# Output sums copied by ScalarE, one transposed load in place of two, and word conversions in another order, in a fused mLSTM and feed-forward kernel

## Chip, cores and metric

The kernel runs on one core of one Trainium2 chip. Its time is in device microseconds. Three runs of the kernel before gave 425.68, 427.31 and 429.06 us; the median is 427.31 us.

## What is computed

An mLSTM cell (4 batches, 8 heads, 768 positions, head size 40), followed by a feed-forward block on its output, laid out as 3072 tokens by 320.

```python
for t in range(S):                       # mLSTM, S = 768, state C (40x40) and n (40) per head
    m_new = np.maximum(f_gate[:, :, t] + m, i_gate[:, :, t])
    f_stab = np.exp(f_gate[:, :, t] + m - m_new)
    i_stab = np.exp(i_gate[:, :, t] - m_new)
    C = f_stab * C + i_stab * outer(vt, kt)
    n = f_stab * n + i_stab * kt
    h_tilde, nq = C @ qt, n @ qt
    y[:, :, t] = sigmoid(o_gate[:, :, t]) * h_tilde / np.maximum(np.abs(nq), 1.0)

h = ((x @ w1) * (x @ w2)) @ w3           # x: y as (3072, 320); w1, w2: 320 x 1024; w3: 1024 x 1024
out = h @ w_out                          # w_out: 1024 x 320
```

The four weights arrive as 64-bit floats, the other inputs as 32-bit floats.

## The kernel before

**Units and steps.** The sequence is cut into units of 128 positions of one batch: 24 units, numbered `n`, four batches to a chunk of positions. One step `s` of the loop at L820 does the scores and the state of unit `s` and the outputs of unit `s - 1`; besides, it does part of the feed-forward block. There are 32 steps; from step 25 on only feed-forward work is left. TensorE's instructions stay in the order of the program (`in_order`, L84), and so do those of the other engines (`keep_order`, L549): an instruction that waits holds up all that stand behind it on its engine.

**The cell.** `quarter_work` (L338) issues the products of a step in quarters of 64 positions: `ph` (weights times values, of unit s - 1), `pi` (queries times the state before), `ss` (scores of unit s) and `pc` (the state's update). They live in two pairs of PSUM banks, `cell`. `outputs` (L419) scales `pi` by a gate into `h` (L423), adds the four quarters of `ph` to it on VectorE (L430), takes max(|nq|, 1) and its reciprocal (L438 to L441), and makes y with the tanh of the output gate (L443, L445); its small operations are spread over the step by `den()`. L397 multiplies scores by the weights `pw`; L404 and L414 update the state, with POOL's `decayed` (L333) between them.

**Weights of the cell.** `pw` starts as a row of U, spread over partitions: by `rows_of_u` (L293, a VectorE transpose) for units below 10, by DMA (`load_u`, L155) after. `weights` (L298) takes eight exponentials on ScalarE, `masks` (L305) masks on POOL, `out_gate` (L269) takes the tanh.

**Keys and queries.** `turn` (L311) turns them: on TensorE with copies by ScalarE (L325) for units below 10, by VectorE's 32x32 transposes (L317) from 10 on. For these, `load_turned` (L141) loads each of the keys' and queries' halves twice, the second time shifted by 32 columns, so that the dimensions 32 to 39 lie where the transposes read: eight DMAs a step, on SP's queue.

**64-bit words.** `fetch` (L211) brings a piece of weights as words; `scale` (L187) scales its two halves on ScalarE (L191, L195), and `to_f32` (L197) joins them on VectorE (L199, L200). `scale_next` and `convert` (L233, L237) take the pieces in the order in which they were fetched. w1 and w2 are cut in two parts of 512 columns, each with their last 64 rows in `wr`. The first part is wanted by step 2, the second (`wr` last) by step 4. In step 3, `rest` (L883) issues two `scale_next`, and `convert` is called twice inside `quarter_work` (`late`, L376 and L409).

**Feed-forward.** `x_trans` (L478) turns y on TensorE for units below 15, after `twice` (L475) has doubled its last 64 columns on POOL. For later units y goes to DRAM and back (`send` L451, `get_back` L462) and is turned by VectorE (`x_turn` L468). `up` (L618) makes pa = x w1 and pb = x w2 for two slices of 128 columns, `up_rest` (L631) adds the last 64 rows and multiplies; its first block is issued in step 2, one in each of the steps 2 to 5, then two. The last three groups of tokens go by seven products instead of eight (`up_by_seven`, L668), whose banks in steps 19 to 24 are those of the cell. w3 and w_out are folded into one matrix in steps 9 to 16 (`w3_mm`, L259), which `ffn_out` and `out_by_seven` apply.

**Step 2.** The part `between` (L892) turns y of the units 0 and 1 and starts `up`. Between the two, `warm(1, small=38)` (L97) issues products of the identity, nobody reads them: one of 128x512 and 38 of 64x64.

PSUM tiles other than `cell` go round four banks (`mps`, L77): the fifth tile asked for waits until the first has been read.

## Time and profile before

| what | value |
|---|---|
| median of three runs | 427.31 us |
| runs | 425.68, 427.31, 429.06 us |
| the profiled execution's span | 425.8 us |
| TensorE's granted clock, mean | 0.996 |
| TensorE idle, 0 to 23 us | 4.5 us |
| TensorE idle, 23 to 60 us | 2.0 us |
| TensorE idle, 60 to 360 us | 2.1 us |
| TensorE idle, 360 us to the end | 3.4 us |
| VectorE's adds of ph (L430), 88 | 28.6 us, 326 ns each |
| ScalarE busy | 150.1 us |
| POOL busy | 154.3 us |
| DMA packets under 512 B | 109360 of 135211 |

The idle times are the lengths of the stages less TensorE's busy time in them. The profiled execution's span is close to the lowest of the three runs, 1.5 us under their median. Busy time of TensorE is modelled from starts of pipelined products, so a busy TensorE needn't be at its peak; where it waits, the line in the order of time names what it waited for in brackets.

### The profile page before, as it was taken

How to read it: one execution, taken by the hardware profiler on the slowest of the kernel's cores; microseconds unless marked ns; L12 is line 12 of the kernel's file. 1: busy time of each engine (PE TensorE's matmuls, PEld its weight loads, DVE VectorE, ACT ScalarE, POOL GpSimd, SP SyncE). 2: the span in 40 equal slices, each digit the busy share in tenths (PEclk: the TensorE clock that was granted, in tenths of full speed). 3: DMA queues.
4: the chain of work that ended last, by engine and by line, in shares of the span. 5: the costliest groups of instructions: out<-in, count | busy, mean ns of one | idle time of the engine just before them, and what ended most of it. 6: DMA issues, size and time to landing. Idle time of an engine off the chain costs nothing.

```text
span 425.8 us, 13079 instructions
## 1 busy us (share of the span) xinstructions
PE 414.1 (97%) x5353; PEld 335.3 (79%) x5353; DVE 313.5 (74%) x635; ACT 150.1 (35%) x404; POOL 154.3 (36%) x211
## 2 busy tenths in 40 slices
PE   7989989999999999999999999999999999999996
PEld 4768878888688788787777778788778879888896
DVE  6676986888949779778736966596868699575971
ACT  4766865567723623630433313032311110210000
POOL 4421342233303303303307751546453587542100
PEclk9989999999999999999999999999999999999999
DMA  8999998598977776985425675756421120000001
GB/s 186 204 173 245 214 144 140 134 193 180 215 183 154 166 182 135 181 164 105 89 80 130 153 141 121 142 133 117 87 44 36 35 39 2 31 2 31 2 32 62
DMA packets 135211, 51.15 MB, mean 120 GB/s; under 512 B 109360, under 2 KB 126960, under 8 KB 135152
## 3 DMA queue, kind: packets, MB, share of 16 engines
q1 hardware_dynamic: 131552, 46.29, 53.9%
q10 hardware_dynamic: 3600, 4.03, 2.7%
q8 instruction: 42, 0.69, 0.7%
q14 instruction: 17, 0.14, 0.1%
HBM read 44.50 MB, written 5.80 MB: 118 GB/s over the span
## 4 chain that ended last, share of the span: by engine, by line
PE 53%; issue 20%; DVE 7%; POOL 7%; SPq 7%; DMA 5%; ACT 1%; POOLq 0%; DVEq 0%
PE cell L92 17%; PE pa L92 12%; PE o L92 8%; PE pb L92 8%; PE p L92 3%; POOL pw L308 3%; SPq L184 3%; DVE w3T L666 2%; PE pt L95 1%; POOL vw L330 1%; SPq L148 1%; DMA raw<-in_moe_w_dram 1%; PE fill L92 1%; POOL raw L659 1%; POOL state L335 1%
## 5 line engine op out<-in xcount | busy, mean ns | idle before, releaser
L335 POOL TENSOR_TENSOR state<-state,decay 128x164 f32<-128x164 f32 x40 | 20.0, 500 | 154.8 <-DVE state L404 129.0
L92 PE MATMUL pa<-xT,w 128*128 128x256 f32 x240 | 60.4, 382 | 0.0
L92 PEld LDWEIGHTS pa<-xT,w 128*128 128x128 f32 x240 | 44.4, 190 | 6.8 <-DVE h L430 0.4
L303 ACT ACTIVATE pw<-pw,aT 128x64 f32<-128x64 f32 x184 | 46.4, 339 | 3.2 <-ACT o_sb L741 1.9
L92 PE MATMUL pb<-xT,w 128*128 128x256 f32 x192 | 45.4, 379 | 0.0
L729 POOL TENSOR_TENSOR ab<-ab,a_sb 128x512 f32<-128x512 f32 x22 | 29.4, 1356 | 32.2 <-DVE ab L684 32.2
L92 PEld LDWEIGHTS pb<-xT,w 128*128 128x128 f32 x192 | 36.4, 190 | 5.0
L711 POOL TENSOR_TENSOR wo<-wo 128x512 f32<-128x512 f32 x22 | 27.4, 1268 | 29.8 <-DVE wo L686 29.8
L92 PE MATMUL pa<-xT,wr 64*64 64x256 f32 x384 | 37.0, 386 | 0.5 <-DVE wr L200 0.5
L92 PE MATMUL wp<-wo,w3T 128*128 128x320 f32 x128 | 35.9, 433 | 1.1 <-DVE ab L639 0.6
L308 POOL TENSOR_SCALAR_AFFINE_SELECT pw<-pw 64x512 f32<-64x512 f32 x48 | 35.8, 746 | 3.0 <-ACT pw L303 1.2
L92 PE MATMUL pb<-xT,wr 64*64 64x256 f32 x384 | 36.4, 380 | 0.0
L92 PE MATMUL cell<-w3o,ab 128*128 128x320 f32 x128 | 35.4, 432 | 0.0
L638 ACT ACTIVATE a_sb<-pa 128x512 f32<-128x512 f32 x24 | 14.3, 598 | 59.0 <-PE pb L92 59.0
L639 DVE TENSOR_TENSOR ab<-pb,a_sb 128x512 f32<-128x512 f32 x24 | 16.4, 688 | 23.2 <-ACT a_sb L638 22.8
L92 PEld LDWEIGHTS wp<-wo,w3T 128*128 128x128 f32 x128 | 23.8, 190 | 10.5 <-DVE ab L639 0.8
L92 PEld LDWEIGHTS cell<-w3o,ab 128*128 128x128 f32 x128 | 24.3, 190 | 9.5
L92 PEld LDWEIGHTS pa<-xT,wr 64*64 64x64 f32 x384 | 18.9, 132 | 15.4 <-issue 8.8
L686 DVE SCALAR_TENSOR_TENSOR a_sb<-pa,wo 128x512 f32<-128x512 f32 x12 | 8.3, 689 | 29.8 <-PE pa L92 29.8
L430 DVE TENSOR_TENSOR h<-cell,h 64x164 f32<-64x164 f32 x88 | 28.6, 326 | 1.6
L92 PE MATMUL po<-w3o,ab 128*128 128x320 f32 x96 | 26.4, 433 | 0.0
L92 PEld LDWEIGHTS po<-w3o,ab 128*128 128x128 f32 x96 | 18.1, 190 | 7.3
(180 smaller groups left out, 846.4 us busy)
## 6 DMA issues: line engine op xcount, KB each, us to landing
raw<-in_moe_w_dram SPq DMA_DIRECT2D x64, 128.0 KB, 3.4
kbuf<-in_k_dram SPq DMA_DIRECT2D x24, 160.0 KB, 4.5
v_all<-in_v_dram SPq DMA_DIRECT2D x24, 160.0 KB, 4.9
o_in<-in_o_gate_dram SPq DMA_DIRECT2D x24, 160.0 KB, 4.8
pw<-U_d SPq DMA_DIRECT2D x28, 128.0 KB, 3.5
raw<-in_moe_w_dram SPq DMA_DIRECT2D x5, 512.0 KB, 6.7
raw<-in_moe_w_out_dram SPq DMA_DIRECT2D x8, 320.0 KB, 4.1
gates<-in_k_dram SPq DMA_DIRECT2D x28, 80.0 KB, 2.5
```

The source lines that it names most:

```text
L92: in_order(nc.tensor.matmul(out, lhsT=lhsT, rhs=rhs, start=start, stop=stop))
L184: nc.sync.dma_start(out=dst, in_=src)
L303: nc.scalar.activation(out=pw[:, h, :], in_=src[:, h, :], func=AF.Exp, bias=aT[:, c, b * H + h:b * H + h + 1])
L308: nc.gpsimd.affine_select(out=pw[r], in_=pw[r], compare_op=OP.is_ge, fill=0.0, base=0, pattern=[[0, H], [1, L]], channel_multiplier=-1)
L335: nc.gpsimd.tensor_tensor(out=new, in0=old, op=OP.mult, in1=decay[:, b * NP:(b + 1) * NP, 2 * c + x:2 * c + x + 1] .to_broadcast([P, NP, D1]))
L430: nc.vector.tensor_tensor(out=part, in0=ph[x][halves[e]], in1=part, op=OP.add)
L638: nc.scalar.mul(out=a_sb, in_=pa, mul=UP ** -2)
L639: nc.vector.tensor_tensor(out=ab_t[gr][j][:, fs[0]:fs[-1] + 1, t0:t0 + a_sb.shape[-1]], in0=pb, in1=a_sb, op=OP.mult)
L666: nc.vector.tensor_tensor(out=dst, in0=p, in1=q, op=OP.subtract)
L686: nc.vector.scalar_tensor_tensor(out=out, in0=p, scalar=UP ** -2, in1=q, op0=OP.mult, op1=OP.add)
L711: aside_by.tensor_tensor(out=kept[j][:, 1:4:2], in0=kept[j][:, 1:3], in1=kept[j][:, 3:4].to_broadcast([128, 2, TH]), op=OP.add)
L729: aside_by.tensor_tensor(out=t[:, f:FO:FH, :], in0=t[:, f:FO:FH, :], in1=a, op=OP.mult)
```

## The change

1. The filler in step 2 is two products of 128x512, and the 38 small ones are gone. `rows_of_u(3)` goes from ahead of the scalings to behind the three conversions there.
2. In step 3 the two scalings and two conversions go from inside the step's work to behind the next unit's turn, exponentials, masks and the gate.
3. For units from 10 on, ScalarE copies the four quarters of `ph` to `h`, VectorE scales `pi` into memory of `y` and adds both once. The ones beside the values are twos; the denominator is max(-r, r) of r = 1/(2 nq), cut at 0.5, in all units.
4. `load_turned` loads once (four DMAs); `shift` copies the eight last dimensions on ScalarE. The memory of those columns is cleared on POOL at step 4.
5. y is stored to DRAM in rows as it stands, by two DMAs in place of four, and read back in pieces of 32 floats in place of 96; the turn writes in another order.
6. w_out's words are joined by POOL, not by VectorE.
7. `x_trans` comes at the end of a step in all steps, ahead of the exponentials; before, from unit 7 on, it came at the start of the next step. In steps 16 to 23 the next unit's exponentials and the gate are issued ahead of the step's quarter work.

```diff
-    def warm(n, m=4, small=0):
+    def warm(n, m=4):
...
-        for i in range(small):
-            r = halves[i % 2]
-            mm(bank[r, 0, 0:L], ident[r, 0:L], ident[r, 0:L])
...
-    N_DIAG = 2
+    N_DIAG, N_OWN = 2, 10
...
-                for j in range(2):
-                    p0, c0 = hip * DP + j * 32, (1 - j) * 32
-                    nc.sync.dma_start(out=dst[p0:p0 + 32, c0:c0 + NP * RAW].rearrange("r (p e) -> r p e", p=NP),
-                                      in_=of.rearrange("p (r f) d -> r p (f d)", f=4))
+                nc.sync.dma_start(out=dst[hip * DP:hip * DP + 32, 32:TB].rearrange("r (p e) -> r p e", p=NP),
+                                  in_=of.rearrange("p (r f) d -> r p (f d)", f=4))
+
+    def shift(n):
+
+        for mem in turned_in[n % 2]:
+            e = mem[:, 32:TB].rearrange("r (g d) -> r g d", d=D)
+            for p0 in (0, DP):
+                nc.scalar.copy(out=e[p0 + 32:p0 + 64, :, 0:D - 32], in_=e[p0:p0 + 32, :, 32:D])
...
-            to_f32(dst, raw)
+            to_f32(dst, raw, nc.gpsimd if dst.shape[-1] == DM else nc.vector)
...
+        before = y[:, 0:H * D1].rearrange("p (h d) -> p h d", d=D1) if n >= N_OWN else h
...
-        for x, e in quarters if n >= N_DIAG else ():
+        if n >= N_OWN:
+            for x, e in quarters:
+                nc.scalar.copy(out=h[halves[x], 0:H // 2] if x == e else h[halves[x], H // 2:H], in_=ph[x][halves[e]])
+        for x, e in quarters if N_DIAG <= n < N_OWN else ():
...
+            if n >= N_OWN:
+                yield
+                V.tensor_tensor(out=h, in0=before, in1=h, op=OP.add)
+                V.reciprocal(out=den, in_=h[:, :, D:D1])
+            else:
+                yield V.reciprocal(out=den, in_=h[:, :, D:D1])
+            yield V.scalar_tensor_tensor(out=den, in0=den, scalar=-1.0, in1=den, op0=OP.mult, op1=OP.max)
+            v = h[:, :, 0:D]
+            yield V.scalar_tensor_tensor(out=v, in0=den.to_broadcast([P, H, D]), scalar=0.5, in1=v, op0=OP.min, op1=OP.mult)
+            yield V.scalar_tensor_tensor(out=y[:, 0:DM].rearrange("p (h d) -> p h d", d=D), in0=o_t.pop(n), scalar=1.0,
+                                         in1=v, op0=OP.add, op1=OP.mult)
...
+        nc.sync.dma_start(out=y_d[n][:, 0:DM], in_=y[:, 0:DM])
+        nc.sync.dma_start(out=y_d[n][:, DM:DM + REM], in_=y[:, KF * P:DM])
...
-        while s >= N_DVE and turned < min(s - 2, NY):
-            x_trans(turned)
-            turned += 1
...
-            if s == 3:
-                scale_next()
-                scale_next()
...
-            rows_of_u(3)
             for _ in range(3):
                 scale_next()
             for n in range(2):
                 x_trans(n)
                 if n == 0:
-                    warm(1, small=38)
+                    warm(2)
             for _ in range(3):
                 convert()
+            rows_of_u(3)
...
+        if NY < s < NU:
+            if s < NU - 1:
+                weights(s + 1)
+            out_gate(s)
         gated = None
         if s <= NU:
-            gated = quarter_work(s, rest, between if s == 2 else None, convert if s == 3 else None)
+            gated = quarter_work(s, rest, between if s == 2 else None, None)
...
+                shift(s + 1)
                 gated = turn(s + 1)
...
+        if s == 3:
+            scale_next()
+            scale_next()
+            convert()
+            convert()
...
+            nc.gpsimd.memset(gates[RG:P, 0:5 * TC], 0.0)
```

More of the change, by code (lines that the diff above doesn't have):

```diff
@@ L127 @@
     KC = KF + 1
-    y_d = [dram.tile([P, 4, KC, 32], FP, name=f"y_d{n}") if n >= NY else None for n in range(NU)]
+    y_d = [dram.tile([P, KC * P], FP, name=f"y_d{n}") if n >= NY else None for n in range(NU)]
     o_t, u_t = {}, {}
@@ L195, in scale, with to_f32 @@
             nc.scalar.activation(out=lo, in_=lo, func=AF.Copy, scale=2.0 ** -29, bias=2.0 ** 23)
-    def to_f32(dst, raw):
-        bits, V = dst.bitcast(U32), nc.vector
-        V.tensor_scalar(out=bits, in0=raw[:, :, 1], scalar1=3, scalar2=None, op0=OP.logical_shift_left)
-        V.tensor_tensor(out=bits, in0=bits, in1=raw[:, :, 0], op=OP.add)
+    def to_f32(dst, raw, adder):
+        bits = dst.bitcast(U32)
+        nc.vector.tensor_scalar(out=bits, in0=raw[:, :, 1], scalar1=3, scalar2=None, op0=OP.logical_shift_left)
+        adder.tensor_tensor(out=bits, in0=bits, in1=raw[:, :, 0], op=OP.add)
     def cols(c0, n):
@@ L241, in convert @@
         if dst is not None:
-            to_f32(dst, raw)
+            to_f32(dst, raw, nc.gpsimd if dst.shape[-1] == DM else nc.vector)
             return
         w3 = wst.tile([128, CW], FP, name="w3", tag="w3")
-        to_f32(w3, raw)
+        to_f32(w3, raw, nc.vector)
         if half == 0:
@@ L422, in outputs @@
         h = sb.tile([P, H, D1], FP, name="h", tag="h")
-        nc.vector.tensor_tensor(out=h.rearrange("p (n two) d -> p two n d", two=2), in0=pi,
+        y = y_t[n] = sb.tile([P, DM + REM], FP, name="y", tag="y")
+        before = y[:, 0:H * D1].rearrange("p (h d) -> p h d", d=D1) if n >= N_OWN else h
+        nc.vector.tensor_tensor(out=before.rearrange("p (n two) d -> p two n d", two=2), in0=pi,
                                 in1=gT[:, c, hs].rearrange("p (n two) -> p two n", two=2).unsqueeze(3)
@@ L437, in steps @@
             V = nc.vector
-            yield V.tensor_scalar(out=den.bitcast(U32), in0=h[:, :, D:D1].bitcast(U32), scalar1=0x7FFFFFFF, scalar2=None,
-                            op0=OP.bitwise_and)
-            yield V.tensor_scalar(out=den, in0=den, scalar1=1.0, scalar2=2.0, op0=OP.max, op1=OP.mult)
-            yield V.reciprocal(out=den, in_=den)
-            e = o_t.pop(n)
-            nc.vector.scalar_tensor_tensor(out=e, in0=e, scalar=1.0, in1=den.to_broadcast([P, H, D]), op0=OP.add, op1=OP.mult)
-            y_t[n] = sb.tile([P, DM + REM], FP, name="y", tag="y")
-            yield nc.vector.tensor_tensor(out=y_t[n][:, 0:DM].rearrange("p (h d) -> p h d", d=D), in0=h[:, :, 0:D],
-                                           in1=e, op=OP.mult)
+            if n >= N_OWN:
[9 more added lines that the diff above has]
+                                         in1=v, op0=OP.add, op1=OP.mult)
         done = steps()
@@ L454, in send @@
         y = y_t.pop(n)
-        for cc in range(KF):
-            nc.sync.dma_start(out=y_d[n][:, :, cc, :], in_=y[:, cc * P:(cc + 1) * P].rearrange("t (i c) -> t i c", c=32))
-        for i in range(0, 4, 2):
-            nc.sync.dma_start(out=y_d[n][:, i:i + 2, KF, :], in_=y[:, KF * P:DM].rearrange("t (i c) -> t i c", c=32))
+        nc.sync.dma_start(out=y_d[n][:, 0:DM], in_=y[:, 0:DM])
+        nc.sync.dma_start(out=y_d[n][:, DM:DM + REM], in_=y[:, KF * P:DM])
     back_t = {}
@@ L464, in get_back @@
         for i in range(4):
-            nc.sync.dma_start(out=back_t[n][32 * i:32 * (i + 1)].rearrange("r m k c -> r m (k c)"),
-                              in_=y_d[n][:, i].rearrange("(m r) k c -> r m (k c)", r=32))
+            nc.sync.dma_start(out=back_t[n][32 * i:32 * (i + 1)],
+                              in_=y_d[n].rearrange("(r m) (k i c) -> i r m k c", r=32, k=KC, i=4)[i])
     def x_turn(n):
@@ L471, in x_turn @@
             x_t[gr] = ffn.tile([128, KC, TG], FP, name="xT", tag="xT")
-        nc.vector.transpose(out=x_t[gr][:, :, j * P:(j + 1) * P].rearrange("c k (m r) -> c k m r", r=32),
+        nc.vector.transpose(out=x_t[gr][:, :, j * P:(j + 1) * P].rearrange("c k (r m) -> c k m r", r=32),
                             in_=back_t.pop(n).rearrange("r m k c -> r k m c"))
@@ L533 @@
     for i in range(NBV):
-        nc.gpsimd.memset(vbuf[i][:, :, D:D1], 1.0)
+        nc.gpsimd.memset(vbuf[i][:, :, D:D1], 2.0)
     for t in state:
@@ L537 @@
     nc.gpsimd.memset(gates[:, 5 * TC:2 * TB], 0.0)
-    nc.gpsimd.memset(gates[RG:P, NP * RAW:TB], 0.0)
     nc.gpsimd.memset(pick, 0.0)
@@ L945 @@
             turned, converted = 2, converted + (4 if s == 2 else 2)
-        if s + 1 < N_DVE:
-            while turned < min(s - 1, NY):
-                x_trans(turned)
-                turned += 1
-            if s not in (1, 2):
-                turn(s + 1)
+        while turned < min(s - 1, NY):
+            x_trans(turned)
+            turned += 1
+        if s + 1 < N_DVE and s not in (1, 2):
+            turn(s + 1)
         if s < NU:
@@ L955 @@
                     weighted(s + 1)
-                weights(s + 1)
+                if s <= NY:
+                    weights(s + 1)
                 if 2 < s < N_DVE:
@@ L959 @@
                 masks(s + 1)
-            if s != 2:
+            if s != 2 and s <= NY:
                 out_gate(s)
+        if s == 3:
[3 more added lines that the diff above has]
+            convert()
         if s in (16, 17):
```

## The prediction

> **What bounds the kernel now.** I read the page first (busy shares, the 40 slices), then TensorE's waits, then its work by stage, then the four compute engines' order of instructions from 14 to 52 us.

> ```profile
> PE 414.1 (97%) x5353; PEld 335.3 (79%) x5353; DVE 313.5 (74%) x635; ACT 150.1 (35%) x404; POOL 154.3 (36%) x211
> ...
> PEclk9989999999999999999999999999999999999999
> DMA  8999998598977776985425675756421120000001
> ```

> TensorE is busy for 414.1 of 425.8 us, VectorE for 74%. The transfers fill the first seven slices (75 us) and no more. A change that relieves VectorE and SyncE can pay only where TensorE waits for them. Of its waits (us in total, times, longest):

> ```profile
> PE cell L92 <- issue: 1.9, 2, 1.5
> ...
> PE px L95 <- DVE y L445: 1.2, 1, 1.2
> ...
> PE pa L92 <- DVE wr L200: 0.5, 1, 0.5
> ```

> With 0.4 us at 243 (w3T, L666) and 0.2 at 356 (wo, L686), and 0.6 at 108 and 0.4 at 8.3, all waits for VectorE come to 3.3 us. The stages (columns: stage, length, busy time of PE, PEld, DVE, ACT, POOL with counts, granted clock, DMA share, GB/s) say where TensorE has no slack and where the clock fell:

> ```profile
> 20.00:23.40 3.40, 2.21 (x52) 1.74 (x52) 2.79 (x8) 2.37 (x8) 2.14 (x4) 1.00 1.22 165
> 23.40:26.80 3.40, 3.40 (x30) 1.90 (x31) 3.02 (x9) 2.79 (x6) 0.50 (x2) 0.50 0.96 146
> ...
> 280.00:335.00 55.00, 55.00 (x702) 43.80 (x701) 40.72 (x93) 11.23 (x31) 27.10 (x28) 1.00 0.38 78
> ```

> From 280 to 335 TensorE has no idle time, and the stages from 60 to 245 are the same but for 1.9 us. After 2.21 busy us in 3.40 the clock was 0.50 for the next 3.4 us. The early places that the change touches, from the order of time (start, length, instruction, idle time ahead), TensorE first, then ScalarE, then VectorE:

> ```profile
> 22.96 0.83 PE L95 MATMUL px<-ident,y 128*128 128x128 f32 x3 [1.19 <-DVE y L445]
> 23.59 4.90 PE L92 MATMUL fill<-ident 128*128 128x512 f32 x78
> ...
> 43.20 1.89 PE L92 MATMUL pa<-xT,w 128*128 128x256 f32 x8
> ...
> 47.33 0.43 PE L92 MATMUL pa<-xT,wr 64*64 64x256 f32 x1 [0.51 <-DVE wr L200]
> ```

> ```profile
> 42.48 0.69 ACT L191 ACTIVATE raw<-raw 128x512 f32<-128x512 f32 x1 [1.20 <-DMA raw<-in_moe_w_dram]
> ...
> 44.48 0.69 ACT L191 ACTIVATE raw<-raw 128x512 f32<-128x512 f32 x1 [0.74 <-DMA raw<-in_moe_w_dram]
> ...
> 46.56 2.04 ACT L303 ACTIVATE pw<-pw,aT 128x64 f32<-128x64 f32 x8
> ```

> ```profile
> 46.54 0.73 DVE L200 CUSTOM_DVE_ANT_0 wr<-raw,wr 128x1024 uint16<-128x1024 uint16 x1
> ```

> The reader is to see the chain at step 4's up-projection: its last weights land at 42.48 and 44.48, ScalarE scales them as they land (ahead of its exponentials at 46.56), VectorE ends the last at 47.27, and TensorE, which waited 0.51 us, goes on at 47.33. This place is paced by transfers that the change doesn't touch (transposed loads are issued from step 8, returned y from step 17).

> **The filler.** Two large fills replace one and 76 small records. The early steps (outputs of unit 0) reorder so that half of y is done in the 0.54 us that VectorE spends waiting for POOL's decay at 20.4, so y(0) comes near 22.0 and not 22.9. The fill then costs 4 records x 0.43 = 1.7 us (a pair takes 0.88 in the chain of waits), not 4.9, and px(1), at 28.41 before, goes when y(1) and POOL's 0.24 us copy are there, near 24.8. ScalarE still scales three word tiles (3 x 1.1 us, to 25.74) before it copies px, so the up-projection starts at 26.5, not 29.67: 3 us ahead. U's rows (0.70 us of VectorE) moved behind three conversions cost nothing: weights(3), which reads them, is wanted only at 45.1.

> **What becomes of the lead.** ScalarE waits for the next words until 33.06 in both kernels and has a_sb of step 2 behind them (34.36), VectorE its product (34.99). TensorE needs the banks which these release: the transposes of step 3 then end at 36.1 (before 39.5). The keys of unit 3 are copied after the scaling of words that land at 36.63 (37.9 to 38.9), so the scores go at 38.95; step 3's product waits for VectorE's conversions until 40.42 and frees the bank at 41.0. Step 4's pa starts at 41.45 (before 43.20), pb at 43.2. Of 3 us 1.75 are left.

> **The fourth step's words.** Both scalings go from ahead of the keys' copies to behind them, the eight exponentials and the gate; both conversions from inside the quarter work to its end, behind U's rows. ScalarE: exponentials 42.1 to 44.1, gate to 44.5 (rows 2.04 and 0.48), two words of 1.2 us: 45.7 and 46.9. VectorE starts the step's product at 40.4; before, from that product (41.32) to U's rows' end (49.36) took 8.0 us, of which the two conversions 2.3, and the shorter denominator saves 0.1: free at 46.1 to 46.4. Conversions of 1.1 to 1.2 us end at 47.4 and 48.5. pb's second product needs the first of them, so TensorE idles from 43.4 to 47.4, needs 1.5 us for pb, and starts the rest at 48.9: 1.6 us behind 47.33. Bounds: -0.5 (landing 44.4 + 1.2 + 1.2 = 46.8, no one in the way) and +2.3 (contended y rows of 0.8 and U's rows later). I take +1.6, the sum of the rows in their order.

> **The clock.** Four idle us must cover most of a 3.4 us window, and 1.19 idle us were enough once. One window at 0.50 costs 1.7 us: bounds 0 (57.50 to 61.00 had 1.49 idle us and the clock held) and 3.4 (two windows). I take 1.7. [...]

> **Steady steps, units 10 on.** Per step VectorE loses four adds (4 x 0.33) and gains one of 0.49 from SBUF; the denominator goes from 0.17 + 0.16 + 0.19 to about 0.39; both large products stay. That is 1.0 us less for 14 steps. ScalarE gains four copies of 164 columns (0.30 each, between the rows of 96 and 384 columns, 0.25 and 0.47) and four shifts of 128 columns (0.27): 2.3 us a step where it is busy 6.5 of 15. SyncE issues four loads less (4 x 0.43) and two y stores less. All of it lies beside a TensorE without idle time: nothing, and if the cover went, at most the 2 us on ScalarE. What waits behind: the turn of keys behind the shifts (VectorE reached it at 147.94, the shifts end near 144), the next scalings behind them (converted at 149.8, scaled by 148.5). Exponentials and gate moved ahead of the copies from step 16: in step 20 they ran 277.49 to 279.9 in any case; the copies end at 281.0 and the bank is written at 281.98. Margin 1.0 us; without it, 0.5 us x 12 steps at worst. w_out's adds: eight of 0.62 us leave VectorE for POOL at 0.74 (nearest row vw, 0.76), which is 64% idle. The memset of gates (32 rows of 1280) is POOL's too, bounds 0 to 3 us, hidden. x_trans goes ahead of the exponentials on ScalarE, with TensorE's order unchanged: 0.

> **Returned y.** Reading comes in pieces of 128 B and not 384, three times the packets: landing between 2.0 us (now) and 6.0; x_turn between 0.57 and 0.83 (scattered write, by the row of 1.10 for 512). The data lay ready 1 to 9 us before use and VectorE idles 4 to 5 us a step: 0; at unit 23, where the chain is tightest, 0 to +1. [...]

> **Other waits.** VectorE's 0.4 at 243 and 0.2 at 356 go with the relief: -0.6. The 1.5 us at 59.05 waits for no engine: an instruction fetch of 16 KB had started at 56.59. With 150 fewer TensorE instructions its place moves: between -1.5 and +1.5, taken 0.

> **Sum**: +1.6 + 1.7 - 0.6 = +2.7. The profiled execution is the low one (span 425.8, runs 425.68 to 429.06); its 428.5 stands 1.5 us below what the median of 427.31 gives: **430.0**.

> **Rivals.**
> 1. Faster than before: the words are in time. If the first conversion ends by 45.8, the rest starts no later than 47.33; at the landing bound it starts 0.5 earlier. For it: ScalarE and VectorE have idle time just before. Against: both queues are in order, and the rows between add up. With the waits at 243 and 356 gone and the fetch stall too, -0.5 - 0.6 - 1.5 = -2.6: 424.7. Chance 0.20.
> 2. ScalarE becomes the bound in the late steps: copies slower than 0.55 us each overrun the margin of 1.0 us, TensorE waits for the cell bank. 0.3 to 0.5 us in 8 to 12 steps is 3 to 4 us over the early loss without the clock's: 427.3 + 1.6 + 4 = 433. Against: the rows of 0.25 and 0.47. Chance 0.13.
> 3. No difference: the words cost 1.6, the clock holds, waits and fetch give it back (-0.6, -1): 427.3. For it: the clock held at 57.5. Chance 0.15.
> The forecast has 0.52, its own range 427.9 to 432.

> **Numbers.** About 1% (4.3 us: 423.0, 431.6) is what a measurement can tell. Slower: a fifth of the forecast (0.10) and most of rival 2 (0.11): 0.21. Faster: a quarter of rival 1: 0.05. Same: 0.74. The range 424.7 to 433.0 holds all but about 0.2.

> **What would show it.** Right: pb of step 4 idle for about 4 us on w by L200, its clock 0.50 behind it, the rest near 49; no waits of TensorE for ScalarE's copies from step 11. Wrong: the rest of step 4 starting before 47.3; the words landing other than at 42.5 and 44.4; TensorE idle at the cell bank after 260 us; x_turn waiting for yb.

## The result, and the profile after

The changed kernel takes 432.61 us (median of 430.88, 431.86, 433.36 and 436.19); in the same set the kernel before takes 426.50. The ratio is 1.0147, interval [1.0101, 1.0192]. A later pair on one chip gave 431.14 against 425.89: 1.0118 [1.0092, 1.0145]. It is slower by 5 to 6 us. The ratios leave out executions over 1.5% above the fastest of their kernel, and the profile of one experiment below, `words_back`, is of such an execution (433.99 us).

The profiled execution has a span of 429.2 us and a time of 430.88, the lowest of the four. The page's busy shares and slices:

```profile
PE 412.9 (96%) x5279; PEld 333.3 (78%) x5279; DVE 299.0 (70%) x561; ACT 182.9 (43%) x516; POOL 166.2 (39%) x219
...
PEclk9999899999999999999999999999999999999999
DMA  8989949499992765944415665526211110000001
```

The relief is there: VectorE is busy 14.5 us less, DMA packets fall from 135211 to 124555. ScalarE is busy 32.8 us more. TensorE is busy 1.2 us less, in a span that is 3.4 us longer, so the time is in its waits (line waited for; us in total, times, longest):

```profile
PE pb L92 <- DVE w L202: 4.5, 1, 4.5
...
PE pa L92 <- DVE w3T L672: 1.4, 1, 1.4
PE cell L92 <- ACT qT L327: 0.9, 1, 0.9
PE cell L92 <- issue: 0.7, 2, 0.5
PE wp L92 <- DVE ab L645: 0.7, 1, 0.7
PE px L95 <- issue: 0.5, 1, 0.5
PE o L92 <- DVE wo L692: 0.5, 1, 0.5
```

Before, two of these lines were:

```profile
PE pa L92 <- DVE w3T L666: 0.4, 1, 0.4
...
PE o L92 <- DVE wo L686: 0.2, 1, 0.2
```

The wait of pb for w is new and the largest. w3T is the memory in which VectorE makes differences of tokens for `up_by_seven` in step 18, wo here that of sums of its products; these two waits, which the relief was to remove, grew from 0.41 to 1.41 and from 0.2 to 0.5. The 1.5 us by "issue" at 59.05 is gone. Step 4 in order of time, on TensorE, ScalarE and VectorE (start, length, instruction, idle time ahead):

```profile
41.25 1.89 PE L92 MATMUL pa<-xT,w 128*128 128x256 f32 x8
42.98 0.59 PE L92 MATMUL pb<-xT,w 128*128 128x256 f32 x2
48.10 2.93 PE L92 MATMUL pb<-xT,w 128*128 128x256 f32 x6 [4.53 <-DVE w L202]
50.96 0.48 PE L92 MATMUL pa<-xT,wr 64*64 64x256 f32 x1
```

```profile
42.03 2.02 ACT L305 ACTIVATE pw<-pw,aT 128x64 f32<-128x64 f32 x8
...
44.31 0.66 ACT L193 ACTIVATE raw<-raw 128x512 f32<-128x512 f32 x1
...
45.96 0.67 ACT L197 ACTIVATE raw<-raw 128x512 uint32<-128x512 uint32 x1
```

```profile
45.73 0.70 DVE L297 STREAM_TRANSPOSE pw<-UT 128x512 f32<-128x512 f32 x1
46.36 0.64 DVE L201 TENSOR_SCALAR w<-raw 128x512 uint32<-128x512 uint32 x1
47.14 0.91 DVE L202 CUSTOM_DVE_ANT_0 w<-raw,w 128x1024 uint16<-128x1024 uint16 x1
...
48.79 0.69 DVE L202 CUSTOM_DVE_ANT_0 wr<-raw,wr 128x1024 uint16<-128x1024 uint16 x1
```

Exponentials stand ahead of the scalings on ScalarE, U's rows ahead of the conversions on VectorE, and TensorE goes on 0.05 us after the first conversion's end (47.14 + 0.91). The stages around the gap (stage, length, busy PE, PEld, DVE, ACT, POOL, granted clock as a share of full speed, DMA share, GB/s) show the clock:

```profile
44.00:47.60 3.60, 0.00 (x0) 0.00 (x0) 3.11 (x7) 2.63 (x6) 2.91 (x6) 1.00 1.10 149
47.70:51.00 3.30, 2.90 (x10) 1.88 (x10) 1.65 (x3) 0.00 (x0) 0.67 (x1) 0.50 1.01 296
```

After 3.6 us without one matmul the next 3.3 us have clock 0.50: the six products of pb take 2.93 us. The rest of step 4 starts at 50.96, 3.6 us behind the 47.33 of before.

The tally by profiles (span +3.4): rest of step 4 +3.6, w3T +1.0, wo +0.3, new fetch stalls ("issue" in the lists, where TensorE waits for nothing that the profile shows; that it waits for its instructions is the author's reading of the 16 KB transfers on the instruction queue, q8, of which one has ended 1.2 to 1.7 us ahead of the end of each such wait in these two profiles) at 160 and 207 +1.0; fetch stalls gone at 59, 96 and 145 -2.3. That is +3.6, within 0.2 of the spans. The two profiles thus account for about half of the loss between the medians: by their times they are about 3 us apart (430.88 against about 427.8, the span of 425.8 and the 2.0 us by which its executions exceed their spans).

### The profile page after: what moved, and what is told of

The parts are those of the page before. It is cut to its first block, busy times and chain, and to the rows that moved or that the text cites. A ratio compares the mean times of both kernels' runs of the same rounds, so it can differ in the third digit from the quotient of the medians.

```text
span 429.2 us, 12925 instructions
## 1 busy us (share of the span) xinstructions
PE 412.9 (96%) x5279; PEld 333.3 (78%) x5279; DVE 299.0 (70%) x561; ACT 182.9 (43%) x516; POOL 166.2 (39%) x219
## 2 busy tenths in 40 slices
DMA packets 124555, 46.54 MB, mean 108 GB/s; under 512 B 104721, under 2 KB 116305, under 8 KB 124497
## 4 chain that ended last, share of the span: by engine, by line
PE 79%; SPq 8%; DVE 6%; DMA 2%; issue 2%; ACT 1%; POOL 0%; DVEq 0%; POOLq 0%; ACTq 0%
PE cell L92 21%; PE pa L92 18%; PE pb L92 13%; PE wp L92 8%; PE o L92 8%; PE po L92 6%; SPq L136 4%; PE p L92 3%; SPq L186 2%; DMA raw<-in_moe_w_dram 2%; PE px L95 1%; SPq L155 1%; DVE pw L776 1%; PE pt L95 1%; DVE w3T L672 1%
## 5 line engine op out<-in xcount | busy, mean ns | idle before, releaser
L337 POOL TENSOR_TENSOR state<-state,decay 128x164 f32<-128x164 f32 x40 | 23.8, 595 | 146.8 <-DVE state L406 120.5
L92 PE MATMUL pa<-xT,w 128*128 128x256 f32 x240 | 60.4, 382 | 0.0
L92 PE MATMUL pb<-xT,w 128*128 128x256 f32 x192 | 47.0, 388 | 4.5 <-DVE w L202 4.5
L92 PEld LDWEIGHTS pa<-xT,w 128*128 128x128 f32 x240 | 44.4, 190 | 6.4
L305 ACT ACTIVATE pw<-pw,aT 128x64 f32<-128x64 f32 x184 | 46.4, 337 | 5.0 <-ACT o_sb L747 2.7
L92 PEld LDWEIGHTS pb<-xT,w 128*128 128x128 f32 x192 | 37.2, 194 | 10.1 <-DVE w L202 4.9
L92 PE MATMUL pa<-xT,wr 64*64 64x256 f32 x384 | 37.0, 386 | 0.0
L92 PE MATMUL pb<-xT,wr 64*64 64x256 f32 x384 | 36.4, 380 | 0.0
L92 PE MATMUL wp<-wo,w3T 128*128 128x320 f32 x128 | 35.7, 433 | 0.7 <-DVE ab L645 0.7
L310 POOL TENSOR_SCALAR_AFFINE_SELECT pw<-pw 64x512 f32<-64x512 f32 x48 | 33.3, 694 | 7.9 <-ACT pw L305 5.1
L92 PE MATMUL cell<-w3o,ab 128*128 128x320 f32 x128 | 35.4, 432 | 0.0
L92 PEld LDWEIGHTS cell<-w3o,ab 128*128 128x128 f32 x128 | 24.3, 190 | 9.5
L92 PEld LDWEIGHTS wp<-wo,w3T 128*128 128x128 f32 x128 | 23.8, 190 | 9.9 <-DVE ab L645 0.9
L92 PEld LDWEIGHTS pa<-xT,wr 64*64 64x64 f32 x384 | 19.0, 133 | 15.2 <-issue 9.4
L92 PE MATMUL po<-w3o,ab 128*128 128x320 f32 x96 | 26.4, 433 | 0.0
L92 PEld LDWEIGHTS po<-w3o,ab 128*128 128x128 f32 x96 | 18.1, 190 | 7.3
L434 ACT COPY h<-cell 64x164 f32<-64x164 f32 x56 | 16.2, 290 | 16.7 <-DVE y L427 16.0
```

Source lines behind the costliest of these rows:

```text
L92: in_order(nc.tensor.matmul(out, lhsT=lhsT, rhs=rhs, start=start, stop=stop))
L305: nc.scalar.activation(out=pw[:, h, :], in_=src[:, h, :], func=AF.Exp, bias=aT[:, c, b * H + h:b * H + h + 1])
L310: nc.gpsimd.affine_select(out=pw[r], in_=pw[r], compare_op=OP.is_ge, fill=0.0, base=0, pattern=[[0, H], [1, L]], channel_multiplier=-1)
L337: nc.gpsimd.tensor_tensor(out=new, in0=old, op=OP.mult, in1=decay[:, b * NP:(b + 1) * NP, 2 * c + x:2 * c + x + 1] .to_broadcast([P, NP, D1]))
L434: nc.scalar.copy(out=h[halves[x], 0:H // 2] if x == e else h[halves[x], H // 2:H], in_=ph[x][halves[e]])
```

## Experiments

The theory at first: words put last in step 3 make TensorE idle and drop its clock, and nearly all of the loss is there. Rivals: the loss is the cut filler's (clock, or fetch stalls that move), or it is ScalarE's new work late in the kernel. Where a set has a mean at full clock, it is over the executions whose mean granted clock is 0.999 or 1.0; for the kernel before this mean is 425.7, 425.7 and 425.9 us in the three sets.

### Words back in their place (words_back, from the changed kernel)

```diff
+            if s == 3:
+                scale_next()
+                scale_next()
...
-            gated = quarter_work(s, rest, between if s == 2 else None, None)
+            gated = quarter_work(s, rest, between if s == 2 else None, convert if s == 3 else None)
...
-        if s == 3:
-            scale_next()
-            scale_next()
-            convert()
-            convert()
```

> The changed kernel, with the two scalings and two conversions of step 3 where the kernel before has them (inside the step's work). Theory (late words and the clock behind them): pb of step 4 goes on without a wait of over 1 us, its last 64 rows start at 46.8 to 47.4 and not at 50.9, no window at half clock behind them, and the median falls by 3.6 us or more, to 427 to 429. Rival (the steady steps pay: VectorE waits for ScalarE's copies, ScalarE's queue is fuller): the early place improves but the end doesn't, 431 to 433.

429.38 us, ratio 1.0066 [1.0033, 1.0099]; at full clock 427.0 (four executions). A good half of the loss is recovered. But 0.66% is left, just above what was expected. TensorE's waits, in the profile (433.99 us):

```profile
PE cell L92 <- issue: 3.9, 3, 2.0
PE pt L95 <- issue: 2.9, 1, 2.9
...
PE pa L92 <- DVE w3T L672: 1.4, 1, 1.4
```

No wait for words is left, but this profile alone doesn't show that: the fetch stall of 2.9 us stands just ahead of step 4's up-projection, which starts at 47.08 (its last rows at 52.99, not near 47 as expected), and hides such a wait. Of the runs below with the words in the same place and the short filler, `adds_back` has no wait for them, behind one of 1.6 us for the turned queries, and `copies_first` has 0.8 and 1.3 us. The w3T wait is still there, so it is not the words'. The other executions have a mean clock under 1.0 in five of nine cases: something still drops the clock; in this profile the two slow stretches go with the fetch stalls of 2.0 us (to 20.87) and 2.9 us (to 46.27).

### Only the words last (words_last, from the kernel before)

```diff
-            if s == 3:
-                scale_next()
-                scale_next()
...
-            gated = quarter_work(s, rest, between if s == 2 else None, convert if s == 3 else None)
+            gated = quarter_work(s, rest, between if s == 2 else None, None)
...
+        if s == 3:
+            scale_next()
+            scale_next()
+            convert()
+            convert()
```

> The kernel before, with only the two scalings and two conversions of step 3 moved to the step's end. Theory: the second product of pb in step 4 waits for the word by L200 until about 48, an idle time of 2.5 to 4.5 us, a window at half clock follows, and the time is 3 to 5 us over the kernel before: 429.5 to 431.5. Rival (steady steps): within 1 us of the kernel before.

432.16 us, ratio 1.0138 [1.0090, 1.0187]. TensorE in step 4, and the stage behind it:

```profile
44.20 0.59 PE L92 MATMUL pb<-xT,w 128*128 128x256 f32 x2
50.03 2.93 PE L92 MATMUL pb<-xT,w 128*128 128x256 f32 x6 [5.24 <-DVE w L200]
52.89 0.69 PE L92 MATMUL pa<-xT,wr 64*64 64x256 f32 x1
```

```profile
48.60:55.40 6.80, 5.37 (x54) 3.65 (x55) 2.54 (x4) 0.42 (x1) 1.55 (x3) 0.50 1.18 276
```

This one edit costs nearly what the whole change costs. Without the shorter filler the wait is longer (5.24 against 4.53), and the clock stays at 0.50 for 6.8 us. The place and the mechanism are shown. The edits do not add up, though: this one costs 1.38%, and `words_back` leaves 0.66% of 1.47%.

### Only the filler and U's rows (short_fill, from the kernel before)

```diff
-            rows_of_u(3)
...
-                    warm(1, small=38)
+                    warm(2)
...
+            rows_of_u(3)
```

> The kernel before, with only the filler of step 2 cut to two large products and U's rows moved behind the three conversions. Theory (step 4 is paced by the words' landing at 42.5 and 44.4): step 2's up-projection starts about 2 to 3 us sooner, TensorE waits for kT, banks and wr later, the last rows of step 4 start at 46.8 to 47.4 as before, and the time is within 1 us of the kernel before. Rival 1 (the filler's time is saved): 2 to 3 us faster, 423.5 to 424.5. Rival 2 (idle time in place of filler halves the clock behind step 4): 1 to 2 us slower.

429.28 us, ratio 1.0062 [1.0025, 1.0099]: not the neutral edit that was expected. Its profiled execution is a good one (426.56) and has the wait that paced step 4 before:

```profile
46.02 0.43 PE L92 MATMUL pa<-xT,wr 64*64 64x256 f32 x1 [0.55 <-DVE wr L200]
```

Step 2's up-projection starts 2.3 us sooner than before (27.35 against 29.67), the last rows of step 4 1.3 us sooner (46.02 against 47.33), and half of that is the words' landing itself, 0.6 to 0.7 us earlier in this execution (41.88 and 43.78 against 42.48 and 44.48). So the landing takes up most of the lead. The executions differ in the clock: two of ten at full clock, the others 426.6 to 431.6 at 0.992 to 0.996, one at 0.980. Of the kernel before, 42 of 65 executions were at full clock. But the clock is only a part of the loss: the two at full clock take 427.1 on average, 1.4 us more than the kernel before at full clock, and the profile doesn't show where.

### The gap filled (gap_filled and, in a later set, gap_filled_again; from the changed kernel)

Five products of the identity stand in the bank of pb ahead of its own in step 4.

```diff
+            if p is pb and gr == 0 and fs[0] == 4 and cs.start == 0:
+                for _ in range(5):
+                    mm(pb.rearrange("p i (a b) -> p (i a) b", a=2), ident, ident.unsqueeze(1).to_broadcast([P, 4, P]))
```

> The changed kernel, with five products of the identity, 4.4 us, written to pb's bank ahead of pb in step 4, where TensorE otherwise waits for the word; they are overwritten. Theory (the idle time costs twice, once as a wait and once as a window at half clock): the word is there as before near 48, the clock stays at 1.0, the last rows start near 49.5 in place of 50.9, and the time is 1.0 to 2 us below the changed kernel's, still 3 us over the kernel before. Rival (the clock is no part of it): no difference from the changed kernel, or slower by the products that don't fit, 0 to 1 us.

> The changed kernel with five products of the identity in the place where TensorE waits for the word, once more, beside the changed kernel. Theory (the idle time costs twice): most executions at clock 1.0, median 1.0 to 2.0 us under the changed kernel. Rival (the clock is no part of it): within 0.5 us of the changed kernel.

First 431.31 us, ratio 1.0112 [1.0025, 1.0200]; then 430.14, 1.0097 [1.0064, 1.0130], beside 431.14 for the changed kernel in the same set (`after_again`). Order of time and stages in the first:

```profile
42.88 4.46 PE L92 MATMUL pb<-ident 128*128 128x512 f32 x10
47.17 2.13 PE L92 MATMUL pb<-xT,w 128*128 128x256 f32 x8
```

```profile
44.00:47.00 3.00, 3.00 (x8) 1.33 (x7) 2.51 (x7) 2.59 (x5) 2.36 (x4) 1.00 0.69 108
47.00:50.00 3.00, 2.90 (x21) 1.73 (x23) 2.21 (x3) 0.00 (x0) 1.65 (x3) 1.00 1.12 222
```

With the same late words and a busy TensorE the clock holds from 47.9 on in both profiles, where in both of the changed kernel's it is at 0.50 there (from 47.68 and from 46.80): with the 4.5 us of idle time filled, the drop is gone. The gain is 1.0 us by the medians of the second set, with overlapping intervals. The clock is not secured: most executions were expected at full clock, two of four and one of six were. In the repeat's profile a fetch stall of 1.84 us ends at 42.29, and the clock is at 0.50 from 41.1 to 47.9 all the same.

> The changed kernel once more, beside the next one on the same chip. Theory: every execution has at least one window at half clock behind step 4 (mean clock 0.996 or lower), median 431 to 433.5.

`after_again`: 431.14 us, and no execution of six at full clock (0.988 to 0.996). Its profile has the pb wait at 4.46 us, and behind it a slow stretch twice as long as in the first profile, 6.8 us (46.8 to 53.6):

```profile
47.50:51.00 3.50, 1.90 (x5) 1.54 (x6) 2.71 (x4) 0.18 (x1) 1.72 (x3) 0.50 1.15 255
51.00:54.50 3.50, 3.50 (x68) 2.18 (x67) 0.00 (x0) 0.53 (x1) 0.00 (x0) 0.62 1.06 287
```

### Filler and rows back too (early_back, from words_back)

`warm(1, small=38)` and `rows_of_u(3)` return to where they stood in the kernel before.

> The changed kernel with its whole early part as before: words inside step 3, filler of one large and 38 small products, U's rows ahead of the conversions; the rest (copies by ScalarE, single loads, returned y, order of exponentials) stays changed. Theory (the filler's removal costs what words_back left open, since idle time that took its place drops the clock in many executions): mean clock 0.995 to 1.0 in nearly all executions, median 1.0 to 1.7 us over the kernel before, 2 to 3 us under words_back; TensorE's wait at w3T stays 1.4 us. Rival (the late steps cost what was left open): as words_back, 3 to 4 us over the kernel before.

426.84 us, ratio 1.0013 [0.9980, 1.0046]; nine of twelve executions at full clock. At full clock it is 426.7, 1.0 above the kernel before. Its waits name this rest:

```profile
PE pa L92 <- DVE w3T L675: 1.4, 1, 1.4
...
PE o L92 <- DVE wo L695: 0.5, 1, 0.5
```

### VectorE's adds back (adds_back, from words_back)

```diff
-    N_DIAG, N_OWN = 2, 10
+    N_DIAG, N_OWN = 2, 24
```

No unit takes the new copies; the quarters of `ph` are added by VectorE as before.

> words_back with VectorE's four adds in place of ScalarE's copies for all units. Theory (the copies stand behind exponentials on ScalarE and VectorE waits for them 1.7 us in step 18): TensorE's wait at w3T falls from 1.4 to 0.4 to 0.7 us, the time 0.7 to 1.2 us under words_back at the same clock. Rival (the relief is worth something elsewhere): TensorE gets new waits after 100 us, time as words_back or over it.

425.74 us, ratio 0.9990 [0.9961, 1.0019]; at full clock 425.4 against 427.0 for `words_back`. The filler is still the short one here. Of the two waits one remains in the list, at its old size; w3T is no longer in it:

```profile
PE o L92 <- DVE wo L692: 0.2, 1, 0.2
```

The two waits are about 1.5 us shorter together, close to the 1.6 us that the time at full clock falls. That the copies make the w3T wait is shown; how, the changed kernel's step 18 tells. ScalarE first, then VectorE, then TensorE:

```profile
232.29 2.02 ACT L305 ACTIVATE pw<-pw,aT 128x64 f32<-128x64 f32 x8 [0.47 <-ACT o_sb L747]
234.22 0.45 ACT L272 ACTIVATE o_in<-o_in 128x320 f32<-128x320 f32 x1
234.57 1.18 ACT L434 COPY h<-cell 64x164 f32<-64x164 f32 x4
```

```profile
235.78 0.50 DVE L447 TENSOR_TENSOR h<-y,h 128x328 f32<-128x328 f32 x1 [1.74 <-ACT h L434]
...
244.41 1.48 DVE L672 TENSOR_TENSOR w3T<-xT,w3T 128x256 f32<-128x256 f32 x1
```

```profile
245.94 0.70 PE L92 MATMUL pa<-w3T,w 128*128 128x256 f32 x2 [1.41 <-DVE w3T L672]
```

Before, VectorE added straight from the bank:

```profile
230.91 1.34 DVE L430 TENSOR_TENSOR h<-cell,h 64x164 f32<-64x164 f32 x4
```

Now its one add waits 1.74 us for copies that stand behind the next unit's exponentials on ScalarE. From the scaling of `pi` to the end of w3T VectorE took 12.4 us in this step (230.37 to 242.77 in the kernel before); now it takes 13.4 (232.49 to 245.89), the 1.0 us that TensorE waits longer.

### Copies ahead of the exponentials (copies_first, from words_back)

In steps 16 to 23 `weights(s + 1)` and `out_gate(s)` go back behind the quarter work.

> words_back with the exponentials and the gate of steps 16 to 23 issued behind the quarter work again, so that the copies stand ahead of them on ScalarE. Theory (order on ScalarE's queue): VectorE's wait for the copies in step 18 falls from 1.7 us to under 0.5, TensorE's wait at w3T from 1.4 to under 0.3, time 1.0 to 1.4 us under words_back at the same clock. Rival (the copies themselves are late, by their length): the wait at w3T stays over 1 us.

429.85 us, ratio 1.0103 [1.0058, 1.0148]; at full clock 429.6, 2.6 more than `words_back`. The expectation failed. TensorE's waits:

```profile
PE cell L92 <- ACT wo L708: 1.8, 5, 0.4
...
PE pa L92 <- DVE wr L202: 1.3, 1, 1.3
...
PE pb L92 <- DVE w L202: 0.8, 1, 0.8
...
PE pa L92 <- DVE w3T L672: 0.4, 1, 0.4
```

The w3T wait falls to 0.4 (under 0.3 was expected), and VectorE takes 12.4 us from the scaling of `pi` to the end of w3T as before (229.49 to 241.87): the order on ScalarE's queue made that wait. But now ScalarE's kept copies (L708) free the cell banks too late: the second rival's mechanism, made by the opposite order. These five waits cost more than the 1.8 us listed. From the first product with w3T to the one that waits for wo, TensorE takes 116.8 us here (241.93 to 358.75) and 113.7 in `words_back` (248.99 to 362.65). That is 3.16 us lost, and 2.1 of the 2.6 us once the 1.02 gained at w3T is taken off. The waits for words, 2.1 us, are early, where the edit changes nothing. The words land as in the kernel before: ScalarE starts on them at 42.65 and 44.95 (42.48 and 44.48 before, 42.50 and 44.64 in `adds_back`), and step 4 goes on at 47.56 (47.33 before).

### Which filler matters (large_fill and small_at_front, from the kernel before)

`large_fill` has `warm(5)` in step 2, as long as the old filler but without the 76 small records; `small_at_front` has that and moves the small ones to the fill at the kernel's start.

> The kernel before with five large products as filler in step 2, 4.4 us at full clock, in place of one large and 38 small ones. Theory (the filler's length matters: it keeps TensorE busy while others work up the lead): within 0.7 us of the kernel before, mean clock 0.995 to 1.0 in most executions. Rival (the number of small instructions matters, since it shifts where instruction fetches fall): 2 to 3 us slower, as short_fill.

428.31 us, ratio 1.0063 [1.0033, 1.0094]; at full clock 427.3. Filler of the old length costs what the short one does: the filler's length is not the cause. More than half of the loss stands at full clock here too (427.3 against 425.7).

> The kernel before, with the 38 small products moved from step 2 to the very first filler (one large product of the two there makes room), and five large ones as filler in step 2. The program of TensorE has again as many instructions ahead of step 3 as the kernel before, within ten. Theory (the count of instructions ahead matters, through where instruction fetches fall, not what runs in step 2): within 0.8 us of the kernel before. Rival (small products in that place do something that large ones don't): 2 to 3 us slower, as large_fill.

435.18 us, ratio 1.0211 [1.0169, 1.0253]: far outside both expectations. The old number of instructions ahead doesn't bring the old time back, so the number alone is not the cause. This profile has the longest wait by "issue" of all, 3.24 us, and the clock is at 0.50 from 20.7 to 30.9 (TensorE's order of time, and the stage):

```profile
22.41 0.36 PE L92 MATMUL cell<-vw,kbuf 64*40 64x41 f32 x4 [3.24 <-issue]
```

```profile
20.70:30.90 10.20, 8.49 (x61) 5.27 (x62) 5.92 (x16) 4.16 (x8) 2.59 (x6) 0.50 0.89 151
```

The stalls' places differ between the kernels: the profiles with the small products in step 2 (the kernel before, `early_back`, `early_and_adds_back`, `words_last`) each have one of 0.5 to 0.7 us ahead of wp, in the kernel before at 144.57, and so has `small_at_front`. Those with fewer products (`short_fill`, `large_fill`, `words_back`, `adds_back`, `copies_first`) have none of 0.2 us or more there, nor has the changed kernel, whose later ones stand at 160.36 and 206.98. The one of 1.5 us, at 59.05 in the kernel before, has its like only in `early_and_adds_back`. That such stalls cause the clock drops early on is not shown. In `words_back`, `small_at_front` and `gap_filled_again` a drop goes with a stall of 1.8 us or more; in `short_fill` and `large_fill` it comes near 23 us, behind a wait for y (1.0 and 1.4 us), as in the kernel before (1.19), and in `adds_back` at 40.1, behind a wait of 1.6 us for the turned queries.

### All three undone (early_and_adds_back)

`early_back` with `N_OWN` 24: what is left of the change are the single loads with ScalarE's shift, the shorter denominator, the returned y, w_out's adds on POOL, x_trans at the step's end and the exponentials ahead.

> early_back with VectorE's four adds in place of ScalarE's copies for all units. What is left of the change: single loads with ScalarE's shifts, the shorter denominator, y returned in other pieces, w_out's adds on POOL, the turn of y at the step's end, exponentials ahead. Theory (all of that lies beside a busy TensorE): TensorE's wait at w3T 0.4 to 0.7 us, within 0.7 us of the kernel before. Rival (the relief pays once the words and copies are out of the way): 1 to 2 us faster than the kernel before.

425.10 us against 425.89, ratio 0.9975 [0.9951, 0.9999]. It is the fastest version, though only just apart from the kernel before, and 0.3 of its 0.8 us lie outside the span (its times stand 1.8 us over their spans, those of the kernel before 2.1). Along this chain of ratios the loss divides as follows: the rest -0.25%, the copies +0.38% (to 1.0013), filler and rows +0.53% (to 1.0066), words +0.81% (to 1.0147). The steps are differences of ratios whose intervals are 0.3 to 0.5% to each side, and in another order they differ: the words alone cost 1.38%, and if the copies are undone first (`adds_back`), they are worth 0.76% and the filler and rows only 0.15%.

## Why the prediction was right, and where not

The forecast was 430.0 us in a range of 424.7 to 433.0; 432.61 lies in it, near its upper end. It foresaw a loss of 2.7 us; 5 to 6 were measured. The direction and the main cause were foreseen; that the time lies in the range is partly luck. It is outside the forecast's own 427.9 to 432, and the range reaches 433.0 for the sake of the second rival, which did not come.

- **Lead and words: right.** The up-projection of step 2 starts at 25.90 (forecast 26.5), pa of step 4 at 41.25 (41.45), pb at 42.98 (43.2). The last scalings end near 45.5 and 46.6 (45.7 and 46.9), U's rows at 46.43 (46.1 to 46.4). The first conversion ends at 48.05 and not 47.4: its two instructions are 0.14 us apart and take 0.64 and 0.91. TensorE idles 4.5 us (4.0).
- **Clock: right at the place, short as a mean.** One window of 0.50 lies behind the gap, as forecast, and the rest of step 4 starts at 50.96 (48.9 + 1.7 = 50.6). But the profiled execution is the best of its four. The others have mean clocks of 0.992, 0.988 and 0.984, and 431.86, 433.36 and 436.19 us. The term of 1.7 us was sized for one window; its bound of 3.4 (two windows) was named and not taken. By their mean clocks seven of the ten executions in both sets have two or more. `words_last` and `after_again` show two in one piece behind the gap; where they lie in the other executions isn't known.
- **"-0.6" for the waits at 243 and 356: wrong in sign**, +1.0 and +0.3. The step counted the work that VectorE loses, not the wait that it gains: the prediction put the copies "beside a TensorE without idle time" and named the shifts and turns behind them, but not VectorE's own add. In step 18 VectorE has no slack, since w3T comes on top. `adds_back` takes both waits back.
- **The filler: direction of its work right, its price wrong.** The lead came and was mostly eaten, as `short_fill` shows at 46.02. But in the kernel before, leaving the small products out costs 0.6% by itself: clock drops in more executions, and 1.4 to 1.6 us at full clock too; the prediction put the price of this edit at a lead only. Why, stays open: it is not length (`large_fill`) and not count alone (`small_at_front`), and without the copies the price is hardly there (`adds_back`).
- **Fetch stall taken as 0 (-1.5 to +1.5): inside its bounds.** It went from 59 (-1.5); with two others gone and two new the sum is -1.3.
- **"The profiled execution is the low one": wrong reason.** Executions of the kernel before stand 2.0 us over their span, so a span of 425.8 belongs to a time of about 427.8, near the median. The 430.0 amounts to the median plus 2.7 in any case.
- **Steady steps, returned y, w_out on POOL: 0, right.** Copies take 290 ns (0.30 us forecast), shifts 295 (0.27), the add 0.56 us on average (0.49), x_turn 0.90 (0.57 to 0.83), reading y back 2.6 (2.0 to 6.0). No wait at the cell banks after 260 us. `early_and_adds_back` puts all of the remaining edits at -0.25%.
- **Rivals.** In time (1): refuted, the first conversion ends at 48.05 and not by 45.8, and the rest starts at 50.96 and not by 47.33. ScalarE late (2): not in the changed kernel, but `copies_first` makes it. No difference (3): refuted, the clock did not hold.

## What to carry to other kernels

Moving work off a busy engine paid nothing here, where another is the bound, and it cost time as soon as the new owner's queue held the work behind something else (VectorE waits 1.74 us in step 18): ask what the relieved engine will now wait for, in the step where it has the least slack. Work that the bottleneck wants next goes ahead of work wanted later on every in-order queue it passes, as the words ahead of exponentials and U's rows. Here a gap of 4.5 us on the bound engine cost its length and a stretch at clock 0.50 behind it (3.4 us, 6.8 in `after_again`), and leaving out products that nobody reads cost 0.6% by itself (`short_fill`): measure such an edit alone, and again with the other edits, since its price here depended on these.
